# A Mamba-2 scan feeding a maxout FFN: decay rows laid out anew through DRAM, and the y matmuls of the seam in three portions

## The chip, the core and the metric

The kernel runs on one core of a Trainium2 chip. The core has TensorE (PE, matmuls), VectorE (DVE), ScalarE (ACT), GpSimd (POOL) and SyncE (SP), which here only issues DMAs; ScalarE issues a few as well. The engines run side by side and meet at semaphores. The metric is the device time of one execution in microseconds (us), lower is better: the median of the runs timed without the profiler. The profile is one further execution, with its own span.

## The reference

Two stages. The first is a scan over the sequence in chunks, with decays `a`; the second is a feed-forward layer with the maximum of three products.

```python
log_a = log(clip(a, 1e-6, 1))                        # a: (4 batches, 8 heads, 768)
for each chunk of the sequence:
    cum = cumsum(log_a in the chunk)
    L = exp(cum_i - cum_j) for i >= j, else 0
    y = ((C B^T) * L) x  +  (C state) * exp(cum)      # x: (4, 8, 768, 32); B, C: (4, 8, 768, 16)
    state = exp(sum of log_a) * state + sum_j B_j x_j exp(cum_last - cum_j)
t = y as (3072 tokens, 256)
h = max(t @ w1, t @ w2, t @ w3)                       # w: (256, 768)
out = h @ w_out                                       # (768, 256)
```

The kernel works in blocks of 128 tokens of all four batches and all eight heads: six blocks, c = 0 to 5. The blocks from c = 1 on are scanned in two halves (u) of 64 tokens. The index i is that of the token that receives, j that of the token that sends.

## The kernel before

At the start come small loads: block 0's decays (a0, four copies), B, C and x of block 0 and three pieces of the weights. The decays of all blocks (a_sb) are six loads on ScalarE's queue. They stand in the program after the logarithm of a0 and before fj0.

```python
a0 = const.tile([P, P], FP32, name="a0")
for k in range(REP):
    eng = nc.sync if k % 2 == 0 else nc.scalar
    eng.dma_start(out=a0[k * BH:(k + 1) * BH], in_=a_rows[:, 0:P])
a_sb = const.tile([R, 2, P], FP32, name="a_sb")          # R = 96 rows, twice
# ... activation table, loads, constants
spread_mask(b)                                            # b = 0, 1: first TensorE work
clip(cum0)                                                # cum0 is a0
lg0 = logs(cum0, "lg0")                                   # ScalarE: L264
for c in range(NC):
    w, k = divmod(c * BH, R)
    nc.scalar.dma_start(                                  # L378
        out=a_sb[k:k + BH, w], in_=a[:, :, c * P:(c + 1) * P].rearrange("b h i -> h b i"))
running(P, lg0, cum0, keep)                               # DVE scan: L269
# ...
fj0 = from_last(BH, cum0, "fj0")                          # ScalarE: L278
spread_i((0, 1), False)                                   # TensorE: L333
from_j[0] = by_token(BH, fj0, "from_j0", 1.0, ffn_bank)   # TensorE transpose: L287
spread_j((0, 1))                                          # TensorE: L345
```

The logarithms and running sums of a_sb go to DRAM (cums), and from there, copied to many partitions, to the decay matrices L (one for each block from c = 1) and to E (the decays that scale C and the states).

```python
scan_c(0)
lg = logs(a_sb, "lg")
running(R, lg, a_sb, keep2)
for w in range(2):
    nc.sync.dma_start(                                    # L960
        out=cums.rearrange("u c h b i -> u (c h b) i")[:, w * R:(w + 1) * R].rearrange(
            "u r i -> r u i"),
        in_=a_sb[:, w].rearrange("r (u i) -> r u i", u=2))
fetch()                                                   # a weight piece, 512 KB
decay_load(1, (0,))
fetch()
decay_load(1, (1,))
for _ in range(3):
    fetch()
load(1, "B")
load(1, "C")
fetch()
last_load(1)                                              # E
```

The masks (decay_masks, GpSimd, L406), exponentials (decay_part, ScalarE, L416) and products with the scores (scan_weight, DVE, L564) work on L with heads outside, batches inside. Then y of a block is made in two steps on TensorE, both of very short matmuls:

```python
def scan_old(c):                                          # L576: 32 matmuls
    # from the states (state of the block, and the middle state) and the scaled C
def scan_own(c):                                          # L592: 64 matmuls
    for b in range(NB):
        for h in range(NH):
            t, q = divmod(h, QH)
            for u in range(2):
                rows = slice(u * HP, (u + 1) * HP)
                nc.tensor.matmul(
                    out=st["y"][t][u][q * D:(q + 1) * D, b],
                    lhsT=st["x"][rows, b * NH + h], rhs=M[rows, h, b], ...)
```

The seam is the place between block 0 and the rest. The feed-forward of block 0 runs as 18 groups (n = 0 to 17), beside which the weights are decoded and block 1 is prepared. Then follow:

```python
for n in range(NF * 3):
    # ... one group of 2 matmuls 128x512 (L652), maximum on DVE (L1064), decode() and sign() of weights
    if n == 14:
        later.extend(scan_state(1, att_bank))             # the states, finished on GpSimd (L522)
    # ...
    if n == 17:
        decode()
        weight_sums(1)
shared["ffn"] = False
scan_old(1)
scan_own(1)
scan_y(1)                                                 # ScalarE copies y: L619
scan_sums(1)                                              # DVE sums of it: L627
pop(9)
transposed(2, False)                                      # trB: L435
scan_bd(2)
add_downs(0)
down_next()                                               # one output piece of block 0: L888
```

From there the feed-forward of a block c runs in nine steps, each of seven products 128x256 (L702; a Strassen form with sums on DVE), with the scan of block c + 1 in between.

Of the kernel before, what the change touches and what calls it, by code (L numbers as in the profile page):

```python
# [19 lines left out]
def kernel(  # L20
# [23 lines left out]
    nc = tc.nc  # L44
# [61 lines left out]
        eng.dma_start(out=a0[k * BH:(k + 1) * BH], in_=a_rows[:, 0:P])  # L106

    a_sb = const.tile([R, 2, P], FP32, name="a_sb")

    tabs = list(get_activation_tables(nc.m.arch).keys())  # L110
    nc.scalar.add_instruction(
# [187 lines left out]
        return scaled(turned(rows, src, name, bank), name, scale)  # L299

    L0 = att.tile([P, NB, NH, P], FP32, tag="L0", bufs=1, name="L0")
    Ls = {}

    def decays(c):
        Ls[c] = att.tile([P, NH, NB, HP], FP32, tag="L", name="L")
        return Ls[c]


# [62 lines left out]
    cum0 = a0.unsqueeze(1)  # L373
    clip(cum0)
    lg0 = logs(cum0, "lg0")
    for c in range(NC):
        w, k = divmod(c * BH, R)
        nc.scalar.dma_start(  # L378
            out=a_sb[k:k + BH, w], in_=a[:, :, c * P:(c + 1) * P].rearrange("b h i -> h b i"))
    running(P, lg0, cum0, keep)  # L380
    ncum[0] = by_token(BH, cum0, "ncum0", -1.0, ffn_bank)


    cums = dram.tile([2, NC, NH, NB, HP], FP32, name="cums")

    def decay_load(c, gs=(0, 1)):
        L = decays(c) if 0 in gs else Ls[c]
        for g in gs:
            h = slice(g * HALF, (g + 1) * HALF)
            for u in range(2):  # L390
                nc.sync.dma_start(
                    out=L[u * HP:(u + 1) * HP, h].rearrange("j h b i -> j (h b i)"),
                    in_=cums[u, c, h].rearrange("h b i -> (h b i)").partition_broadcast(HP))

    def last_load(c):
        E = blocks[c]["E"] = raw.tile([HN, 2, NB, HP], FP32, tag="E", name="E")
        for h in range(NH):
            nc.sync.dma_start(
                out=E[h * N:(h + 1) * N].rearrange("n u b i -> n u (b i)"),
                in_=cums[:, c, h].rearrange("u b i -> u (b i)").partition_broadcast(N))  # L400

    def decay_masks(c, g):

        h = slice(g * HALF, (g + 1) * HALF)
        for rows, base in ((P, HP), (HP, 0)):
            nc.gpsimd.affine_select(  # L406
                out=Ls[c][0:rows, h], in_=Ls[c][0:rows, h],
                pattern=[[0, HALF], [0, NB], [1, HP]], compare_op=ALU.is_ge, fill=MASKED,
                base=base, channel_multiplier=-1)

    def decay_part(c, r, b0):

        L = Ls[c]
        for b in (b0, b0 + 1):
            for h in (2 * r, 2 * r + 1):
                nc.scalar.activation(  # L416
                    L[:, h, b], L[:, h, b], AF.Exp,
                    bias=ncum[c][:, h * NB + b:h * NB + b + 1], scale=1.0)


    states = {}
# [43 lines left out]
    def scan_bd(c):  # L465
        st = blocks[c]
        st["Bd"] = Bd = att.tile([P, BH, N], FP32, tag="Bd", bufs=1, name="Bd")
        f = from_j[c].rearrange("p (b h) -> p b h", h=NH) if c == 0 else \
            from_j[c].rearrange("p (h b) -> p b h", b=NB)
        nc.gpsimd.tensor_tensor(  # L470
            out=Bd.rearrange("p (b h) n -> p b h n", h=NH),
            in0=st["B"].rearrange("p (b h) n -> p b h n", h=NH),
            in1=f.unsqueeze(3).to_broadcast([P, NB, NH, N]), op=ALU.mult)

    def first_state(kind):
        st = blocks[0]
# [83 lines left out]
        return banks  # L560

    def scan_weight(c, r, s):
        M = Ls[c][:, 2 * r:2 * r + 2].rearrange("p h b i -> p b h i")
        nc.vector.tensor_tensor(out=M, in0=s, in1=M, op=ALU.mult)  # L564

    def scan_old(c):
# [13 lines left out]
                        start=(b == 0), stop=False, tile_position=(r * PN, q),  # L580
                        skip_group_check=True)

    def scan_own(c):

        st = blocks[c]
        M = Ls[c]
        for b in range(NB):
            for h in range(NH):
                t, q = divmod(h, QH)
                for u in range(2):  # L590
                    rows = slice(u * HP, (u + 1) * HP)
                    nc.tensor.matmul(  # L592
                        out=st["y"][t][u][q * D:(q + 1) * D, b],
                        lhsT=st["x"][rows, b * NH + h], rhs=M[rows, h, b],
                        start=False, stop=True, tile_position=(u * HP, q * D),
                        skip_group_check=True)

# [83 lines left out]
    def weight_sums(k):  # L681
        q, i = divmod(k, 3)
        a11, a12, a21, a22 = (
            w_sb[i][:, kk, (2 * q + g) * P:(2 * q + g + 1) * P]
            for g in range(2) for kk in range(2))
        s1, s2, s3, s4 = (wsum[k][:, j] for j in range(4))
        nc.gpsimd.tensor_tensor(out=s1, in0=a21, in1=a22, op=ALU.add)
        nc.gpsimd.tensor_tensor(out=s3, in0=a11, in1=a21, op=ALU.subtract)
        nc.gpsimd.tensor_tensor(out=s2, in0=s1, in1=a11, op=ALU.subtract)
        nc.gpsimd.tensor_tensor(out=s4, in0=a12, in1=s2, op=ALU.subtract)  # L690
# [265 lines left out]
    scan_c(0)  # L956
    lg = logs(a_sb, "lg")
    running(R, lg, a_sb, keep2)
    for w in range(2):
        nc.sync.dma_start(  # L960
            out=cums.rearrange("u c h b i -> u (c h b) i")[:, w * R:(w + 1) * R].rearrange(
                "u r i -> r u i"),
            in_=a_sb[:, w].rearrange("r (u i) -> r u i", u=2))
    fetch()
    decay_load(1, (0,))
    fetch()
    decay_load(1, (1,))
    for _ in range(3):
        fetch()
    load(1, "B")  # L970
    load(1, "C")
# [29 lines left out]


    def decay_list(c):
        return [(c, r, b0) for r in range(NP) for b0 in (0, 2)]

    parts = {c: decay_list(c) for c in range(1, NC)}

# [5 lines left out]
    def first_tokens():  # L1013
        from_js = by_token(R, fj, "from_js", 1.0, att_bank)
        for c in range(1, NC):
            ncum[c], from_j[c] = (t[:, c * BH:(c + 1) * BH] for t in (ncums, from_js))

    def loads(c):
        if c < NC:
            if c == 3:  # L1020

                load(c, "x")
                decay_load(2, (1,))
                load(2, "x")
            decay_load(c)
            last_load(c)
            load(c, "B")
            load(c, "C")
            if c > 3:
                load(c, "x")  # L1030
# [10 lines left out]
    for n in range(NF * 3):  # L1041
        j, g = divmod(n, 2)
        q, i = divmod(j, 3)
        f = 2 * q + g
        if n == 0:
            pair = [ffn_bank([P, BLK], "up") for _ in range(2)]
            group(pair[0], 0, 0, (0,))
            first_own((2, 3))
            group(pair[1], 0, 1, (0,))
            for p, ff in zip(pair, range(2)):  # L1050
                group(p, 0, ff, (1,))
        if j > 0:
            p = ffn_bank([P, BLK], "up")
            whole_group(p, i, f)
        else:
            p = pair[g]
        if i == 0 and g == 0:
            m = ffn.tile([P, 4, HB], FP32, tag="m", name="m")
        pop({13: 2, 14: 1, 15: 2, 16: 1}.get(n, 0))
        mg = m[:, 2 * g:2 * g + 2].rearrange("p r t -> p (r t)")  # L1060
        if i == 0:
            nc.scalar.copy(out=mg, in_=p)
        else:
            nc.vector.tensor_tensor(  # L1064
                out=mg if i == 1 else h_of(0)[:, f], in0=mg, in1=p, op=ALU.max)
        if g == 0 and n <= 16:
            sign()
            if n <= 14:
                decode()
        if n == 1:  # L1070
            fj = from_last(R, a_sb, "fj", HP)
        if n == 3:
            first_tokens()
            load(2, "B")
            fetch()
            load(2, "C")
            fetch()
            decay_load(2, (0,))
            last_load(2)
            home(2, "x")  # L1080
            decay_masks(1, 0)
        if n == 5:
            decay_masks(1, 1)
        if n in (5, 7, 9, 10, 11, 12, 13, 14):
            part(1)
        if n == 11:
            transposed(1)
            scan_bd(1)
            scan_c(1)
        if n == 12:  # L1090
            scan_e(1)
            scan_cd(1)
            scores(1)
        if n == 14:
            later.extend(scan_state(1, att_bank))
        if n == 15:
            shared["att"] = False
            places()
            weight_sums(0)
        if n == 17:  # L1100
            decode()
            weight_sums(1)
    shared["ffn"] = False
    scan_old(1)
    scan_own(1)
    scan_y(1)
    scan_sums(1)
    pop(9)
    transposed(2, False)
    scan_bd(2)  # L1110
    add_downs(0)
    down_next()


# [4 lines left out]
    P1 = [(1, 0, 0), (1, 0, 0), (1, 0, 1), (1, 1, 1), (0, 0, 1), (1, 1, 2), (1, 0, 0), (1, 0, 2),  # L1119
          (1, 0, 2)]  # L1120
    D1 = [(0, 0), (0, 0), (2, 0), (2, 0), (2, 0), (2, 0), (0, 2), (0, 1), (0, 2)]
    K1 = {0: (0, 0), 1: (0, 1), 3: (1, 0), 5: (1, 1)}
    X2 = ["t", "s", "AD", "D", "D", "y", "D", "D", "D"]
    Y2 = ["", "", "", "D", "", "", "", "", ""]
    P2 = [(1, 0, 1), (1, 1, 2), (0, 0, 2), (1, 0, 1), (1, 0, 0), (1, 0, 0), (9, 0, 0), (1, 0, 0),
          (1, 0, 0)]
    D2 = [(0, 0), (2, 0), (1, 0), (0, 0)] + 5 * [(0, 1)]
    K2 = {2: (1, 0), 3: (1, 1)}
    X3, Y3, P3 = 9 * [""], 9 * [""], 9 * [(1, 0, 0)]

    for c in range(1, NC):
# [97 lines left out]
```

## Time and profile before

| | before |
|---|---|
| time, median of 3 | 311.21 us (311.11 to 311.37) |
| span of the profile | 311.2 us |
| TensorE busy | 287.4 us (92%), 3004 passes |
| VectorE busy | 208.3 us (67%) |
| ScalarE busy | 112.2 us (36%) |
| GpSimd busy | 121.9 us (39%) |
| moved by DMA | 23.02 MB, mean 74 GB/s |
| a_sb loads, ScalarE's queue | 6, of 16 KB |
| cums stores | 2, of 48 KB, 1.5 us to landing |
| decay loads (L from cums) | 20, of 256 KB, 5.2 us to landing |
| E loads (from cums) | 40, of 32 KB, 3.2 us to landing |

An engine's busy share is a mean over the span. The page also cuts the span into 40 slices of 7.8 us and gives the busy tenths of each; an empty slice of TensorE is worth more attention than the mean. The timeline gives for every instruction its start, its duration, and in brackets how long its engine had been idle and what released it. The chain of work that ended last goes back from the last instruction, at each step to what released it.

### The profile page before, as it was taken

The numbers are of one execution on the slowest core, as the hardware profiler recorded it, in microseconds if no ns is written. First come the engines' busy times: TensorE is split into PE (matmuls) and PEld (weight loads), VectorE is DVE, ScalarE is ACT, GpSimd is POOL, SyncE is SP. The second block draws the span as 40 slices with busy tenths as digits, with TensorE's granted clock in tenths as the row PEclk, the third lists the DMA queues.
The fourth block names the chain that finished last, engine by engine and source line by source line (L and its number), as shares of the span: only waits on it lengthen the run. The fifth ranks groups of instructions, "written<-read, shape, count | busy, mean of one in ns | idle before, by whom it ended". The sixth has DMA issues, their size and how long they took to land.

```text
span 311.2 us, 7425 instructions
## 1 busy us (share of the span) xinstructions
PE 287.4 (92%) x3004; PEld 230.5 (74%) x3004; DVE 208.3 (67%) x414; ACT 112.2 (36%) x335; POOL 121.9 (39%) x143
## 2 busy tenths in 40 slices
PE   5098998999699999999999999999999999999995
PEld 3075563445588888778898788898789878988885
DVE  2036448768376886987677678576886687586682
ACT  2037275692254553470333533342621211110111
POOL 4013328347549959193600293300625042130300
PEclk9999999999699999999999999999999999999999
DMA  8914997999577000279000478100100100000102
GB/s 84 231 44 118 214 211 161 176 206 147 71 171 74 29 3 2 87 149 106 19 19 2 134 113 95 38 2 0 36 2 0 38 0 34 3 0 0 36 1 101
DMA packets 84962, 23.02 MB, mean 74 GB/s; under 512 B 75904, under 2 KB 80576, under 8 KB 84928
## 3 DMA queue, kind: packets, MB, share of 16 engines
q1 hardware_dynamic: 84448, 22.29, 39.1%
q8 instruction: 23, 0.38, 0.5%
q10 hardware_dynamic: 480, 0.26, 0.3%
q14 instruction: 11, 0.09, 0.1%
HBM read 19.30 MB, written 3.24 MB: 72 GB/s over the span
## 4 chain that ended last, share of the span: by engine, by line
PE 79%; DVE 11%; DMA 2%; issue 2%; SPq 2%; ACT 1%; POOL 1%; ACTq 0%; DVEq 0%; POOLq 0%
PE sumB L702 24%; PE sumA L702 17%; PE o L812 13%; PE up L652 6%; PE o L888 3%; DMA raw_x<-in_x_dram 2%; PE y L592 2%; PE s L556 2%; PE s L537 2%; PE y L576 2%; DVE rb L627 2%; PE up L644 2%; DVE rb L744 1%; PE y L604 1%; PE spread L333 1%
## 5 line engine op out<-in xcount | busy, mean ns | idle before, releaser
L702 PE MATMUL sumA<-yT,w 128*128 128x256 f32 x180 | 55.5, 389 | 0.2
L787 POOL TENSOR_TENSOR hs<-h 128x256 f32<-128x256 f32 (+1 forms) x8 | 9.2, 1149 | 101.5 <-DVE h L747 101.5
L702 PE MATMUL sumB<-rb 128*128 128x256 f32 x180 | 46.7, 382 | 0.0
L727 ACT COPY eu<-sumA 128x256 f32<-128x256 f32 x45 | 16.8, 373 | 72.7 <-PE sumA L702 56.6
L416 ACT ACTIVATE L<-L,ncums 128x64 f32<-128x64 f32 x160 | 41.4, 340 | 4.0 <-POOL L L406 4.0
L702 PEld LDWEIGHTS sumB<-rb 128*128 128x128 f32 x180 | 34.7, 193 | 4.9
L702 PEld LDWEIGHTS sumA<-yT,w 128*128 128x128 f32 x180 | 31.0, 192 | 5.2 <-issue 1.0
L191 POOL TENSOR_TENSOR w_u<-w_u,w_r 128x512 uint32<-128x512 uint32 x12 | 15.2, 1270 | 39.6 <-DVE w_u L185 30.0
L652 PE MATMUL up<-yT,w 128*128 128x512 f32 x64 | 29.3, 601 | 1.5 <-DVE w L194 1.4
L744 DVE TENSOR_TENSOR rb<-sumB,eu 128x512 f32<-128x512 f32 x30 | 20.7, 692 | 12.6 <-PE sumB L702 12.4
L702 PE MATMUL sumB<-yT,rb 128*128 128x256 f32 x90 | 28.1, 393 | 1.2 <-DVE m L730 0.6
L728 DVE TENSOR_TENSOR eu<-sumA,eu 128x256 f32<-128x256 f32 x45 | 18.9, 421 | 15.1 <-ACT eu L727 14.8
L702 PE MATMUL sumA<-rb 128*128 128x256 f32 x90 | 27.2, 385 | 0.0
L702 PE MATMUL sumB<-rb,w 128*128 128x256 f32 x90 | 26.8, 379 | 0.0
L406 POOL TENSOR_SCALAR_AFFINE_SELECT L<-L 128x1024 f32<-128x1024 f32 (+1 forms) x20 | 24.7, 1233 | 0.7
L652 PEld LDWEIGHTS up<-yT,w 128*128 128x128 f32 x64 | 11.6, 190 | 15.9 <-issue 10.9
L729 DVE TENSOR_TENSOR v<-sumB,eu 128x256 f32<-128x256 f32 x45 | 19.1, 425 | 5.4 <-PE sumB L702 0.5
L702 PEld LDWEIGHTS sumB<-yT,rb 128*128 128x128 f32 x90 | 15.8, 189 | 7.6 <-DVE m L730 3.3
L702 PEld LDWEIGHTS sumA<-rb 128*128 128x128 f32 x90 | 17.4, 193 | 2.4
L702 PEld LDWEIGHTS sumB<-rb,w 128*128 128x128 f32 x90 | 17.1, 190 | 2.3
L812 PE MATMUL o<-wo,h 128*128 128x128 f32 x120 | 17.6, 280 | 0.6 <-DVE ob L821 0.6
L812 PEld LDWEIGHTS o<-wo,h 128*128 128x128 f32 x120 | 15.9, 191 | 2.8 <-ACT eu L727 1.1
(141 smaller groups left out, 507.8 us busy)
## 6 DMA issues: line engine op xcount, KB each, us to landing
L<-cums SPq DMA_DIRECT2D x20, 256.0 KB, 5.2
rb<-in_moe_w_dram SPq DMA_DIRECT2D x9, 512.0 KB, 8.4
raw_x<-in_x_dram SPq DMA_DIRECT2D x6, 512.0 KB, 6.6
out_dram<-ob SPq DMA_DIRECT2D x11, 256.0 KB, 2.2
raw_B<-in_B_dram SPq DMA_DIRECT2D x6, 256.0 KB
raw_C<-in_C_dram SPq DMA_DIRECT2D x6, 256.0 KB, 6.2
rb<-in_moe_w_out_dram SPq DMA_DIRECT2D x3, 512.0 KB, 6.0
E<-cums SPq DMA_DIRECT2D x40, 32.0 KB, 3.2
```

The source lines that it names most:

```text
L191: nc.gpsimd.tensor_tensor(out=u, in0=u, in1=r, op=ALU.add)
L406: nc.gpsimd.affine_select(out=Ls[c][0:rows, h], in_=Ls[c][0:rows, h], pattern=[[0, HALF], [0, NB], [1, HP]], compare_op=ALU.is_ge, fill=MA ...
L416: nc.scalar.activation(L[:, h, b], L[:, h, b], AF.Exp, bias=ncum[c][:, h * NB + b:h * NB + b + 1], scale=1.0)
L652: nc.tensor.matmul(out=bank, lhsT=w_sb[i][:, k, f * P:(f + 1) * P], rhs=yT[0][:, k], start=(k == 0), stop=(k == KD - 1))
L702: nc.tensor.matmul(out=bank[:, half], lhsT=left(p, k), rhs=sides[c][p], start=(first and half == 0), stop=True, skip_group_check=True)
L727: nc.scalar.copy(out=eu[:, 0], in_=A[:, 0])
L728: nc.vector.tensor_tensor(out=eu[:, 1], in0=A[:, 1], in1=eu[:, 0], op=ALU.add)
L729: nc.vector.tensor_tensor(out=v, in0=B[:, 1], in1=eu[:, 1], op=ALU.add)
L744: nc.vector.tensor_tensor(out=t[:, 0:2], in0=B, in1=eu[:, 1:2].to_broadcast([P, 2, HB]), op=ALU.add)
L787: eng.tensor_tensor(out=s1, in0=a21, in1=a22, op=ALU.add)
L812: nc.tensor.matmul(out=o[:, PLACES[p]], lhsT=token_sums[c][p][:, f, u], rhs=wo_of(p)[:, f], start=(p == first and f == 0), stop=True, skip ...
L888: nc.tensor.matmul(out=o[:, i], lhsT=hT[0][:, f, b * P:(b + 1) * P], rhs=wo_sb[:, f], start=(f == 0 and i == 0), stop=True, skip_group_che ...
```

## The change

Two things are changed.

The decay rows. a_sb is loaded in one transfer, ahead of the activation table, with batch and head outside and the block inside (row = (batch, head), block). For the layout that the decay loads need, the sums go to DRAM as they are (rows_dram) and two transfers from DRAM to DRAM, one for each half of a block, write cums anew. L now has batches outside and heads inside, so the decay loads, masks and exponentials go by pairs of batches instead of halves of the heads. The E loads take runs of 64 numbers instead of 256. The purpose is to free ScalarE's queue of the six loads, and to let scan_own begin with the first two batches.

The seam. scan_old(1) goes after group n = 16, scan_own(1) of batches 0 and 1 after n = 17, then one output piece of block 0, then scan_own(1) of batches 2 and 3. The short matmuls so stand in three portions with long ones in between. The number of matmuls stays; one output piece moves here from a later step.

```diff
     a_sb = const.tile([R, 2, P], FP32, name="a_sb")
+    nc.scalar.dma_start(
+        out=a_sb,
+        in_=a_rows.rearrange("r (c i) -> (r c) i", i=P).rearrange("(w r) i -> r w i", w=2))
...
-        Ls[c] = att.tile([P, NH, NB, HP], FP32, tag="L", name="L")
+        Ls[c] = att.tile([P, NB, NH, HP], FP32, tag="L", name="L")
...
-    for c in range(NC):
-        w, k = divmod(c * BH, R)
-        nc.scalar.dma_start(
-            out=a_sb[k:k + BH, w], in_=a[:, :, c * P:(c + 1) * P].rearrange("b h i -> h b i"))
     running(P, lg0, cum0, keep)
...
-    cums = dram.tile([2, NC, NH, NB, HP], FP32, name="cums")
+    rows_dram = dram.tile([BH, NC, P], FP32, name="rows_dram")
+    cums = dram.tile([NC, 2, NB, NH, HP], FP32, name="cums")
...
     def last_load(c):
...
-                out=E[h * N:(h + 1) * N].rearrange("n u b i -> n u (b i)"),
-                in_=cums[:, c, h].rearrange("u b i -> u (b i)").partition_broadcast(N))
+                out=E[h * N:(h + 1) * N].rearrange("n u b i -> n (u b) i"),
+                in_=cums[c, :, :, h].rearrange("u b i -> (u b) i").partition_broadcast(N))
...
-    def scan_own(c):
+    def scan_own(c, bs=range(NB)):
...
-    for w in range(2):
+    nc.sync.dma_start(
+        out=rows_dram.rearrange("k c s -> (k c) s").rearrange("(w r) s -> r w s", w=2), in_=a_sb)
+    fetch()
+    for u in range(2):
         nc.sync.dma_start(
-            out=cums.rearrange("u c h b i -> u (c h b) i")[:, w * R:(w + 1) * R].rearrange(
-                "u r i -> r u i"),
-            in_=a_sb[:, w].rearrange("r (u i) -> r u i", u=2))
+            out=cums[:, u].rearrange("c b h i -> c (b h) i"),
+            in_=rows_dram[:, :, u * HP:(u + 1) * HP].rearrange("k c i -> c k i"))
     fetch()
     decay_load(1, (0,))
     fetch()
-    decay_load(1, (1,))
-    for _ in range(3):
+    decay_load(1, (2,))
+    for _ in range(2):
         fetch()
...
+        if n == 16:
+            scan_old(1)
         if n == 17:
             decode()
             weight_sums(1)
+            scan_own(1, (0, 1))
     shared["ffn"] = False
-    scan_old(1)
-    scan_own(1)
+    add_downs(0)
+    down_next()
+    scan_own(1, (2, 3))
     scan_y(1)
     scan_sums(1)
     pop(9)
     transposed(2, False)
     scan_bd(2)
-    add_downs(0)
     down_next()
```

Left out of this cut: the same change of layout in the decay loads, masks, exponentials and the scaling of B; the order in which the parts of the exponentials are taken; and the tables of which mask runs in which step.

More of the change, by code (lines that the diff above doesn't have):

```diff
@@ L375, with decay_load @@
     lg0 = logs(cum0, "lg0")
-    for c in range(NC):
-        w, k = divmod(c * BH, R)
-        nc.scalar.dma_start(
-            out=a_sb[k:k + BH, w], in_=a[:, :, c * P:(c + 1) * P].rearrange("b h i -> h b i"))
     running(P, lg0, cum0, keep)
     ncum[0] = by_token(BH, cum0, "ncum0", -1.0, ffn_bank)
-    cums = dram.tile([2, NC, NH, NB, HP], FP32, name="cums")
[L386 to L389, printed above, removed]
+    rows_dram = dram.tile([BH, NC, P], FP32, name="rows_dram")
+    cums = dram.tile([NC, 2, NB, NH, HP], FP32, name="cums")
+    def decay_load(c, pairs=(0, 2)):
+        L = decays(c) if 0 in pairs else Ls[c]
+        for b in pairs:
             for u in range(2):
                 nc.sync.dma_start(
-                    out=L[u * HP:(u + 1) * HP, h].rearrange("j h b i -> j (h b i)"),
-                    in_=cums[u, c, h].rearrange("h b i -> (h b i)").partition_broadcast(HP))
+                    out=L[u * HP:(u + 1) * HP, b:b + 2].rearrange("j b h i -> j (b h i)"),
+                    in_=cums[c, u, b:b + 2].rearrange("b h i -> (b h i)").partition_broadcast(HP))
     def last_load(c):
@@ L398, in last_load, with decay_masks @@
             nc.sync.dma_start(
-                out=E[h * N:(h + 1) * N].rearrange("n u b i -> n u (b i)"),
-                in_=cums[:, c, h].rearrange("u b i -> u (b i)").partition_broadcast(N))
-    def decay_masks(c, g):
-        h = slice(g * HALF, (g + 1) * HALF)
+                out=E[h * N:(h + 1) * N].rearrange("n u b i -> n (u b) i"),
+                in_=cums[c, :, :, h].rearrange("u b i -> (u b) i").partition_broadcast(N))
+    def decay_masks(c, b0):
+        b = slice(b0, b0 + 2)
         for rows, base in ((P, HP), (HP, 0)):
             nc.gpsimd.affine_select(
-                out=Ls[c][0:rows, h], in_=Ls[c][0:rows, h],
-                pattern=[[0, HALF], [0, NB], [1, HP]], compare_op=ALU.is_ge, fill=MASKED,
+                out=Ls[c][0:rows, b], in_=Ls[c][0:rows, b],
+                pattern=[[0, 2], [0, NH], [1, HP]], compare_op=ALU.is_ge, fill=MASKED,
                 base=base, channel_multiplier=-1)
@@ L416, in decay_part @@
                 nc.scalar.activation(
-                    L[:, h, b], L[:, h, b], AF.Exp,
-                    bias=ncum[c][:, h * NB + b:h * NB + b + 1], scale=1.0)
+                    L[:, b, h], L[:, b, h], AF.Exp,
+                    bias=ncum[c][:, b * NH + h:b * NH + h + 1], scale=1.0)
     states = {}
@@ L467, in scan_bd @@
         st["Bd"] = Bd = att.tile([P, BH, N], FP32, tag="Bd", bufs=1, name="Bd")
-        f = from_j[c].rearrange("p (b h) -> p b h", h=NH) if c == 0 else \
-            from_j[c].rearrange("p (h b) -> p b h", b=NB)
         nc.gpsimd.tensor_tensor(
-            out=Bd.rearrange("p (b h) n -> p b h n", h=NH),
-            in0=st["B"].rearrange("p (b h) n -> p b h n", h=NH),
-            in1=f.unsqueeze(3).to_broadcast([P, NB, NH, N]), op=ALU.mult)
+            out=Bd, in0=st["B"], in1=from_j[c].unsqueeze(2).to_broadcast([P, BH, N]),
+            op=ALU.mult)
     def first_state(kind):
@@ L562, in scan_weight @@
     def scan_weight(c, r, s):
-        M = Ls[c][:, 2 * r:2 * r + 2].rearrange("p h b i -> p b h i")
+        M = Ls[c][:, :, 2 * r:2 * r + 2]
         nc.vector.tensor_tensor(out=M, in0=s, in1=M, op=ALU.mult)
@@ L581, in scan_old @@
                         skip_group_check=True)
-    def scan_own(c):
+    def scan_own(c, bs=range(NB)):
         st = blocks[c]
         M = Ls[c]
-        for b in range(NB):
+        for b in bs:
             for h in range(NH):
@@ L593, in scan_own @@
                         out=st["y"][t][u][q * D:(q + 1) * D, b],
-                        lhsT=st["x"][rows, b * NH + h], rhs=M[rows, h, b],
+                        lhsT=st["x"][rows, b * NH + h], rhs=M[rows, b, h],
                         start=False, stop=True, tile_position=(u * HP, q * D),
@@ L1003, in decay_list @@
     def decay_list(c):
-        return [(c, r, b0) for r in range(NP) for b0 in (0, 2)]
+        return [(c, r, b0) for r, b0 in (
+            (0, 0), (1, 0), (0, 2), (1, 2), (2, 0), (2, 2), (3, 0), (3, 2))]
     parts = {c: decay_list(c) for c in range(1, NC)}
@@ L1015, in first_tokens @@
         for c in range(1, NC):
-            ncum[c], from_j[c] = (t[:, c * BH:(c + 1) * BH] for t in (ncums, from_js))
+            ncum[c], from_j[c] = (
+                t.rearrange("p (k c) -> p c k", c=NC)[:, c] for t in (ncums, from_js))
     def loads(c):
@@ L1022, in loads @@
                 load(c, "x")
-                decay_load(2, (1,))
+                decay_load(2, (2,))
                 load(2, "x")
@@ L1082 @@
         if n == 5:
-            decay_masks(1, 1)
+            decay_masks(1, 2)
         if n in (5, 7, 9, 10, 11, 12, 13, 14):
@@ L1121 @@
     D1 = [(0, 0), (0, 0), (2, 0), (2, 0), (2, 0), (2, 0), (0, 2), (0, 1), (0, 2)]
-    K1 = {0: (0, 0), 1: (0, 1), 3: (1, 0), 5: (1, 1)}
+    K1 = {0: (0, 0), 1: (0, 2), 3: (1, 0), 5: (1, 2)}
     X2 = ["t", "s", "AD", "D", "D", "y", "D", "D", "D"]
@@ L1127 @@
     D2 = [(0, 0), (2, 0), (1, 0), (0, 0)] + 5 * [(0, 1)]
-    K2 = {2: (1, 0), 3: (1, 1)}
+    K2 = {2: (1, 0), 3: (1, 2)}
     X3, Y3, P3 = 9 * [""], 9 * [""], 9 * [(1, 0, 0)]
```

## The prediction

> **What bounds the kernel now.** I read the page's row of engines and its forty slices first, then TensorE's waits, then the timeline around the two largest of them, then a table by stage. TensorE is busy 287.4 of 311.2 us; only its 24 us of idleness, and the time in which it runs slowly, can be won.
>
> The slices and the instruction queues of the page, and TensorE's waits, longest first in total:
>
> ```profile
> PE   5098998999699999999999999999999999999995
> PEclk9999999999699999999999999999999999999999
> DMA  8914997999577000279000478100100100000102
> q8 instruction: 23, 0.38, 0.5%
> q14 instruction: 11, 0.09, 0.1%
> ```
>
> ```profile
> PE from_j_tp L287 <- ACT fj L278: 8.9, 1, 8.9
> PE y L592 <- issue: 3.2, 1, 3.2
> PE spread L317 <- DVE keep L254: 2.5, 1, 2.5
> PE up L652 <- DVE w L194: 1.4, 2, 1.1
> ```
>
> Slice 1 (7.8 to 15.6 us) is empty on TensorE, and slice 10 (78 to 86 us) is the only later one below 8; its clock digit is also the only low one. The waits name both: 8.9 us for an exponential on ScalarE, and 3.2 us at the y matmuls, put down to nothing ("issue"). From slice 11 on TensorE is full, so what is won before about 87 us should move the end by as much.
>
> Why ScalarE is late shows in its timeline (start, duration, then the instruction; ACTq is its DMA issuing; from several windows, so the x3 and x2 rows share one issue):
>
> ```profile
> 3.74 0.31 ACT L264 ACTIVATE lg<-a 128x128 f32<-128x128 f32 x1 [0.71 <-DVE a L259]
> 3.75 2.69 ACTq L378 DMA_DIRECT2D a_sb<-in_a_dram  x3
> 5.76 1.39 ACTq L378 DMA_DIRECT2D a_sb<-in_a_dram  x2
> 10.87 0.67 ACTq L378 DMA_DIRECT2D a_sb<-in_a_dram  x1
> 14.47 0.67 ACTq L378 DMA_DIRECT2D a_sb<-in_a_dram  x1
> 15.19 0.40 ACT L278 ACTIVATE fj<-a 32x128 f32<-32x128 f32 x1 [11.14 <-DMA a_sb<-in_a_dram]
> ```
>
> ScalarE computes nothing from 4.05 to 15.19 us, although its input, the scan of a0, is ready at 4.50 (L269: 4.08 + 0.42). Six small loads of a_sb stand before fj in its program, and the fifth and sixth are held back. The chain of work that ended last says by what: it has the landing of raw_x (7.01 + 7.44 = 14.45), then this issue at 14.47, fj, and the transpose at 15.64. The program's order with its waits agrees: DMAs of both queues take eight completion semaphores in turn, and the sixth a_sb load waits for that of raw_x, the fifth for that of the first weight piece. No bandwidth of its own is missing.
>
> The stages (us; busy time and count of PE, PEld, DVE, ACT, POOL; granted clock; DMA share; GB/s):
>
> ```profile
> 6.74:15.64 8.90, 0.00 (x1) 0.00 (x0) 0.00 (x0) 0.40 (x1) 0.57 (x1) 1.00 1.22 224
> 38.00:75.00 37.00, 35.48 (x238) 17.13 (x234) 27.16 (x44) 25.11 (x65) 18.07 (x16) 1.00 1.01 178
> 77.20:80.40 3.20, 0.04 (x6) 0.04 (x8) 0.00 (x0) 0.00 (x0) 3.12 (x5) 0.90 0.24 55
> 80.40:87.00 6.60, 6.33 (x43) 5.11 (x44) 2.77 (x5) 2.93 (x8) 2.04 (x4) 0.53 0.82 124
> ```
>
> In the second hole DVE and ScalarE are idle too and DMA is almost so. Then TensorE runs 6.6 us at about half clock.
>
> [...] 0.38 MB in 23 packets is 16.5 KB each. An fp32 matmul here is four instructions (two weight loads, two passes), a transpose two. Counting TensorE's program up to the hole, I get 869 before the y stage, 128 for scan_old, and 102 passes with their 102 loads of scan_own: 1201. [...] the hole lies amid scan_own, at no wait of the program, with every other engine's input ready. [...] For the SP-issued cums store of before the trace shows 1.5 us to landing. [...] no run shows the new transfers yet.
>
> **Part 1, decay rows.** Six a_sb loads (11.40 us of ScalarE's queue) become one of 96x2x128, issued after the two a0 loads at about 1.7 us. Those took 0.91 together, so I allow 0.5. The table load (1.28) then ends about 3.5, and the log waits for DVE's clip (3.71) anyway: 0 to 0.6 lost, say 0.2. fj runs at about 4.7 instead of 15.19. TensorE finishes its 32 spread passes at 6.74 and takes from_j_tp at once: 8.9 - 0.2 = 8.7 us earlier. Are the next inputs there 8.7 us earlier? From the bytes by microsecond, raw_B and raw_C are in by about 8.0 us, the first weight piece by 10.3, raw_x by 14.45, two more weight pieces by 16.4. The first needs, moved forward: trB 10.8, trC 13.8, first weight decode 16.4, state product 20.0. All hold, the decode by 6 us.
>
> The layout costs DMA work. Before: two cums stores at 25.71, landing in 1.5, then decay loads at 27.27. After: a rows_dram store at about 17, a weight piece behind it, two DRAM-to-DRAM transfers after its landing (about 19), and the decay loads after theirs (about 22 behind the weight piece) instead of 18.6 in moved time: 3 to 4 us later. Their mask runs on GpSimd at 47.22, moved 38.5, so 12 us are left. Weight pieces 4 to 9 also shift 1 to 2 us, with the same sort of slack (piece 4 issued 26.61, decoded 43.86). The final scaling loads E change from 1 KB to 256-byte runs, 1024 instead of 256 per block. raw_x moved 4096 runs of 128 bytes in about 4 us, so by proportion about 1 us; E is issued at 46.98 and used at 66.66. Hidden. ScalarE's exponentials (160 at 340 ns), masks and scan weights keep number and size. Net: -8.7, less 0.2 for small slips.
>
> **Part 2, y at the seam.** TensorE's order becomes: groups up to n=16, scan_old, group 17, half of scan_own, one output piece, the other half. Nothing is added; one output piece is taken from a later slot. In before's clock: groups 15 and 16 end at 73.1. scan_old then waits for the middle state, which GpSimd finishes at 74.62: about 1.5 us of new wait. Then 1.1 (scan_old), 1.8 (group, four passes), 0.7 (half of scan_own, half of the 1.41 a later block took), 0.9 (piece), 0.7: the end of y at 79.8 [...] Left over: 0.6, y ends at 80.4, against 81.0 before with one piece fewer done (0.86: four passes at 0.216, as eight took 1.73 at 95.57). The hole being short, the clock stays up. Then four ScalarE copies and DVE's four sums (80.86 to 84.0, 3.1 us) still stand before the products; they end at about 83.8 instead of 87.0. Seam: 3.2 + 0.86 = 4.1 us if all works. I count 2.7, since [...] DVE (5.0 of 5 us busy from 70 to 75) may take over.
>
> **Sum.** 311.2 - 8.5 - 2.7 = 300.0 us.
>
> **Rivals.** (a) The early hole is only partly filled: a_sb's issue is slowed beside raw_B's 4096 runs, or the weight stream takes over between 38 and 75 us. For: DMA ran at 178 GB/s there, and before it rested from 16.5 to 25.7, a rest that vanishes. Against: only 1.4 us of waits for decoded weights, and 6 us or more of slack. Gain 4 to 6 instead of 8.7: 303 to 305. (b) The seam stays: [...] the wait for GpSimd grows. Gain 0 there, perhaps -1: 302.7 to 304. For: GpSimd is busy 3.12 of 3.20 us in the hole and sets the middle state. (c) All works and TensorE also warms sooner, since it starts continuous work at 2.5 instead of 15.6: 296 to 298. Against: from 15.64 to about 37 it was almost always busy and its 128x128 transposes still took 0.28 us each (1.11 for four at 19.46), against 0.15 when warm (0.60 for four at 86.97), so the small row tiles seem not to warm it. (d) The extra DRAM hop starves the decay path and costs more than all this: over 311; nothing in the slack speaks for it.
>
> **Range and chances.** (a) or (b) alone stay under 305, the 2% line; both together come to about 307. Range 296.5 to 304.0; faster by over 2% 0.92, within 0.07, slower 0.01.
>
> **What would show it.** Right: slice 1 of TensorE full, fj at about 4.7 us and from_j_tp near 6.9; rows_dram at about 17; decay masks near 38.5 with no DMA wait; TensorE waiting about 1.5 us at scan_old for GpSimd; no slow-clock slice near 70 us. Wrong: fj early but a wait for weights or raw_x taking its place; the "issue" wait of 3 us again among the y matmuls with the clock falling after it; or later slices no longer full.

## The result and the profile after

| | before | changed |
|---|---|---|
| time, median of 4 (us) | 311.16 | 293.42 (292.81 to 294.15) |
| ratio, 95% interval | | 0.943 (0.9406 to 0.9455) |
| span of the profile (us) | 311.2 | 292.4 |
| TensorE busy (us) | 287.4 | 277.6 |
| from_j_tp starts (us) | 15.64 | 6.37 |
| first 128x512 group starts | 41.47 | 23.82 |
| scores of block 2 start (chain) | 101.18 | 82.30 |
| from there to the end of the span | 210.0 | 210.1 |

The change is 17.7 us faster, not 11.2. 300.0 was predicted, with 296.5 as the lower end. The last row says that nothing came from later than 101 us. The third row from below says that 17.65 of the 18.8 us of span were won before 41.47 us, where 8.5 were expected.

The slices of the page after (tenths busy, granted clock, DMA share):

```profile
PE   6899899888999989999999999999999999999995
PEclk9999999999999999999999999999999999999999
DMA  7969989979980007871005971001001001000103
```

No slice of TensorE is empty and the slow slice at the seam is gone. TensorE's waits after, longest first in total:

```profile
PE spread L319 <- DVE keep L257: 2.5, 1, 2.5
PE up L648 <- DVE w L197: 1.4, 2, 1.1
...
PE y L572 <- POOL S L518: 1.2, 1, 1.2
PE o L884 <- DVE wo L197: 1.1, 1, 1.1
...
PE y L588 <- issue: 0.4, 1, 0.4
```

The waits of 8.9 and 3.2 us are gone. Two new ones stand at the seam: scan_old for GpSimd's state (1.2, foreseen as 1.5), and an output piece for its decoded weight (1.1, not foreseen).

That waits alone do not explain it shows when the same work is put side by side. TensorE's timeline of the changed kernel (start, duration):

```profile
4.40 2.17 PE L335 MATMUL spread<-a,pick 32*128 32x128 f32 x32
8.03 1.52 PE L335 MATMUL spread<-a,pick 32*128 32x128 f32 x16
9.48 0.66 PE L434 MATMUL trB<-ident,raw_B 128*128 128x128 f32 x4
19.06 1.13 PE L640 MATMUL up<-yT,w 128*128 128x256 f32 x4 [0.70 <-ACT yT L607]
```

and of the kernel before:

```profile
4.57 2.17 PE L333 MATMUL spread<-a,pick 32*128 32x128 f32 x32
17.52 2.01 PE L333 MATMUL spread<-a,pick 32*128 32x128 f32 x16
19.46 1.11 PE L435 MATMUL trB<-ident,raw_B 128*128 128x128 f32 x4
34.88 2.08 PE L644 MATMUL up<-yT,w 128*128 128x256 f32 x4 [0.70 <-ACT yT L611]
```

trB is 9.98 us earlier, the first up matmul 15.82: many of the matmuls between them run almost twice as fast. In what follows, warm is TensorE at full granted clock, cold at half. At 4.4 us it is cold in both kernels: the same 32 passes take 2.17 us in both. In the changed kernel single passes of `spread` shrink from 416 ns to 270 between 8.3 and 8.9 us, so it is warm from about 8.7 us on instead of about 38.8. The page's clock digits do not show it: both read 9 from the start. The clock record of the changed kernel's trace begins only at 8.71 us and that of before at 38.82; what lies ahead of the record is printed as full.

In some executions of experiments 4 to 6 the mean granted clock was lower (0.971 to 0.988) and the time 3 to 7 us longer; where single times are named these are left out or named apart.

### The profile page after: what moved, and what is told of

The parts are those of the page before. It is cut to its first block, busy times and chain, and to the rows that moved or that the text cites. A ratio compares the mean times of both kernels' runs of the same rounds, so it can differ in the third digit from the quotient of the medians.

```text
span 292.4 us, 7409 instructions
## 1 busy us (share of the span) xinstructions
PE 277.6 (95%) x3004; PEld 223.2 (76%) x3004; DVE 207.8 (71%) x414; ACT 112.1 (38%) x335; POOL 121.8 (42%) x143
## 4 chain that ended last, share of the span: by engine, by line
PE 71%; DVE 12%; DMA 8%; SPq 3%; ACT 2%; issue 2%; POOL 1%; DVEq 0%; ACTq 0%; POOLq 0%
PE sumB L698 25%; PE sumA L698 17%; PE o L808 14%; PE o L884 3%; SPq L134 3%; PE y L588 3%; DMA L<-cums 2%; DMA rb<-in_moe_w_dram 2%; PE y L572 2%; PE s L552 2%; DVE rb L623 2%; DMA rows_dram<-a_sb 1%; DVE L L560 1%; DVE rb L740 1%; PE spread L335 1%
## 5 line engine op out<-in xcount | busy, mean ns | idle before, releaser
L698 PE MATMUL sumA<-yT,w 128*128 128x256 f32 x180 | 54.9, 386 | 0.3 <-DVE eu L724 0.2
L698 PEld LDWEIGHTS sumB<-rb 128*128 128x128 f32 x180 | 34.1, 190 | 5.0 <-DVE rb L623 0.4
L405 POOL TENSOR_SCALAR_AFFINE_SELECT L<-L 128x1024 f32<-128x1024 f32 (+1 forms) x20 | 26.0, 1299 | 0.7
```

The lines of the kernel that those rows point to most:

```text
L405: nc.gpsimd.affine_select(out=Ls[c][0:rows, b], in_=Ls[c][0:rows, b], pattern=[[0, 2], [0, NH], [1, HP]], compare_op=ALU.is_ge, fill=MASKE ...
L698: nc.tensor.matmul(out=bank[:, half], lhsT=left(p, k), rhs=sides[c][p], start=(first and half == 0), stop=True, skip_group_check=True)
```

## The experiments

**1. Is it the clock? The hole filled, in the kernel before.**

```diff
     fj0 = from_last(BH, cum0, "fj0")
     spread_i((0, 1), False)
+    filler = bank("sumB", 2, [P, HALF, P], "filler")
+    for _ in range(34):      # never read
+        nc.tensor.matmul(out=filler.rearrange("p k i -> p (k i)"), lhsT=ident16,
+            rhs=mask.unsqueeze(1).to_broadcast([P, HALF, P]), start=True, stop=True, ...)
     from_j[0] = by_token(BH, fj0, "from_j0", 1.0, ffn_bank)
```

> The kernel before, with 34 filler matmuls 128x512 bf16 on TensorE in the hole ahead of from_j_tp; nothing else moves, ScalarE still reaches fj at about 15.2 us. Clock theory: TensorE is warm when the hole ends, the stretch from from_j_tp to the first up matmul shrinks from 19.2 us to about 12.5, and the time falls by about 7 us, to 304. Rival (the extra gain comes from transfers or other engines that now start earlier): no change, 311. Block theory of the seam: the 68 added instructions move the hole among the y matmuls of scan_own from after 102 passes to after 68; if it is a wait for data it stays after 102.

No interval could be had: the four times are 303.53, 309.6, 310.8 and 314.78 us, beside 308.01 to 313.38 for before. Their mean granted clocks, in the same order, are 0.999, 0.978, 0.971 and 0.956. The profiled execution, the longest of them, tells why. Its stages, TensorE alone (us; busy and count; granted clock; DMA share; GB/s):

```profile
6.40:13.60 7.20, 7.18 (x34) 1.00 1.27 181
13.60:15.75 2.15, 0.00 (x0) 1.00 1.04 332
15.75:16.00 0.25, 0.25 (x5) 0.68 1.08 401
17.00:36.00 19.00, 16.94 (x146) 0.50 0.45 113
39.00:40.00 1.00, 1.00 (x3) 0.63 1.05 385
```

The fill ended 2.15 us too soon, for it ran warm (0.21 us each; the four 128x512 bf16 passes at 2.54 us of the kernel before take 1.86 together). The clock had fallen within 0.25 us of from_j_tp's start (0.68 in that row) and stayed at half until about 39.7 us, although TensorE was busy for 16.94 of the 19 us from 17 to 36. So the cold stretch is real, and this trace, unlike the two before, dates it (that of the seam-only kernel in experiment 5 has it on record too, with no fill). The fastest execution (303.53, mean clock 0.999) is where the clock theory put it, but one execution shows little.

The block theory, which has the place of the hole go with the number of instructions ahead of it on TensorE, had no trace behind it. Its forecast failed as put: the hole in scan_own did not move to 68 passes. It vanished (128 passes in 1.49 us at 76.44), and three later y stages, untouched by the edit, got one each:

```profile
118.08 0.45 PE L592 MATMUL y<-L,raw_x 64*32 64x64 f32 x28 [1.45 <-issue]
198.68 0.42 PE L592 MATMUL y<-L,raw_x 64*32 64x64 f32 x23 [1.73 <-issue]
245.43 0.41 PE L592 MATMUL y<-L,raw_x 64*32 64x64 f32 x19 [1.55 <-issue]
```

They come after 100, 105 and 109 of the 128 passes; before's came after 102. From 112 to 120 us DMA's share was 0.01, so busy DMA is not needed for such a hole.

**2. The hole put back into the changed kernel.** ScalarE copies a small tile onto itself 34 times ahead of fj.

```diff
+    slow = const.tile([P, 64], FP32, name="slow")
+    nc.gpsimd.memset(slow, 0.0)
+    for _ in range(34):
+        nc.scalar.activation(slow, slow, AF.Copy)
     fj0 = from_last(BH, cum0, "fj0")
```

> The changed kernel, with 34 small ScalarE operations ahead of fj that hold it back by about 9 us, so the early hole is back while every transfer stays as changed. Clock theory: TensorE stays cold to the first up matmuls, cost 9 + 7 = 16 us, time about 309. Rival: cost only the 9 us, about 302.

314.4 us (313.7 to 314.85), 21 us over the changed kernel; from_j_tp at 17.31, 10.9 us later. TensorE's timeline shows the slow durations of before again:

```profile
21.13 1.11 PE L434 MATMUL trB<-ident,raw_B 128*128 128x128 f32 x4
36.55 2.08 PE L640 MATMUL up<-yT,w 128*128 128x256 f32 x4 [0.70 <-ACT yT L607]
```

The first 128x512 group starts 19.7 us later than in the changed kernel: 10.9 for the hole and 8.8 beyond. All of the transfers' new order was kept, so the new order of the transfers does not bring those 8.8 us.

**3. Held back and filled.** The same with 50 fill matmuls as in experiment 1.

> The changed kernel with fj held back as in the run before (a hole of about 10.8 us) and the hole filled by 50 matmuls 128x512 bf16 on TensorE. Clock theory: TensorE stays warm, only the 10.8 us are lost, 304 us, ten less than without the fill (314.4). Rival (the rest of the cost of holding fj back is in transfers or other engines): about 314 again.

313.31 us, the median of 20 executions from 308.97 to 318.56: near the rival's 314, but not for the rival's reason. Up to the scores of block 2 it was what the clock theory says: they start at 91.94, against 101.76 held without fill. Afterwards it lost the same again. TensorE's waits of this kernel begin:

```profile
PE y L588 <- issue: 6.0, 4, 2.0
```

Three holes of 1.8 to 2.0 us and one of 0.3, in y stages that had none when fj was held without fill, and the mean clock fell to 0.988. The fill adds 100 instructions and nothing else to TensorE's program.

**4. Filled with 256 instructions.** The fills of 68 and 100 instructions came with new holes in y stages. Here the fill is 128 short matmuls, 256 instructions with a load and a pass each; why this number should do better is not shown. For the held kernel (104 columns twice) and for the kernel before (90 columns twice):

```diff
+    for _ in range(128):
+        nc.tensor.matmul(out=filler[:, 0:2, 0:104], lhsT=ident16,
+            rhs=mask[:, 0:104].unsqueeze(1).to_broadcast([P, 2, 104]), start=True, stop=True, ...)
```

> As the held and filled kernel before, but with 128 short fill matmuls, 256 instructions[...]. Clock and block theory together: the hole of about 11 us costs only itself, 304 to 305 us, and no y stage gets a new hole over 0.6 us. Rival to the block theory (the four late holes of the 50-matmul fill came from something else): holes of 1.5 to 2 us again and about 313.

304.25 and 304.38 us: ten less than held without fill, by useless work on TensorE alone (the other two executions took 310.29 and 310.24, at mean clocks of 0.978 and 0.977). Its timeline:

```profile
20.04 0.66 PE L434 MATMUL trB<-ident,raw_B 128*128 128x128 f32 x4
29.61 1.13 PE L640 MATMUL up<-yT,w 128*128 128x256 f32 x4 [0.70 <-ACT yT L607]
```

No y stage waits for "issue" now; one such wait of 0.9 stands at a sumB product.

> The kernel before with the early hole filled by 128 short matmuls, 256 instructions, up to the moment at which ScalarE delivers fj (from_j_tp still at about 15.7 us). Clock theory: the stretch from from_j_tp to the first 128x512 group shrinks from 25.8 to about 17.5 us and the time falls by 7 to 8.4 us against before. Block theory: the hole of the seam stays where it was, after about 102 passes, and no other y stage gets one. Rival: no change.

302.23 to 302.78 us (a fourth execution took 309.16, at a mean clock of 0.971); ratio to before 0.9713 (0.9679 to 0.9748), with from_j_tp no earlier than before (17.05, the fill overran by a little). The hole at the seam is back in its place, after 101 passes, as the only one of the y stages:

```profile
67.90 1.20 PE L592 MATMUL y<-L,raw_x 64*32 64x64 f32 x101
70.64 0.44 PE L592 MATMUL y<-L,raw_x 64*32 64x64 f32 x27 [1.54 <-issue]
```

The clock runs in one table (us):

| kernel | from_j_tp | from there to the first 128x512 group | time |
|---|---|---|---|
| before | 15.64 | 25.83 | 311.2 |
| before, filled (256) | 17.05 | 16.35 | 302.5 |
| changed | 6.37 | 17.45 | 293.4 |
| changed, held | 17.31 | 26.20 | 314.4 |
| changed, held and filled (256) | 18.03 | 16.35 | 304.3 |

The middle column has two levels, about 26 and about 17, and what chooses between them is whether TensorE was at work just before. At the lower level the changed kernel needs 1.1 us more than the filled ones, which are warm when from_j_tp starts; it is not yet.

**5. The two parts one by one.** The changed rows with the seam of before, and the kernel before with the changed seam (moving the four calls as the diff of the change does, and nothing else).

> The changed decay rows with the seam of before (scan_old, scan_own whole after group 17, output pieces after trB). Theory that most of the seam's gain is given back (the pulled-forward pieces meet a weight that is not decoded): 1 to 1.5 us slower than the changed kernel, about 294.6, with a hole of about 3 us after 102 passes of scan_own and a slow clock after it. Rival (the seam is worth what was predicted): 296 to 297.5.

293.1, 294.46 and 294.97 us (a fourth execution took 298.97); ratio 0.9453 (0.9406 to 0.9499). The hole comes after 103 passes, but is 1.9 us instead of 3.2:

```profile
58.19 1.23 PE L588 MATMUL y<-L,raw_x 64*32 64x64 f32 x103
61.33 0.43 PE L588 MATMUL y<-L,raw_x 64*32 64x64 f32 x25 [1.91 <-issue]
```

The clock then is 0.50 from about 63.1 to 66.5.

> The kernel before with only the seam changed. Given-back theory: 1 to 1.5 us faster than before, about 310. Rival: 307 to 308.5. In both the early hole of 8.9 us and the cold stretch after it stay.

311.74 us; ratio to before 1.0024 (0.9994 to 1.0053): nothing, less than either theory. Its trace shows the cold stretch of the kernel before without any fill (TensorE alone; the columns are those of experiment 1):

```profile
6.25:8.00 1.75, 0.00 (x0) 1.00 1.25 133
9.00:9.50 0.50, 0.00 (x0) 0.73 0.55 164
9.50:10.00 0.50, 0.00 (x0) 0.50 1.05 410
15.78:38.00 22.22, 20.16 (x171) 0.50 0.53 120
40.00:41.00 1.00, 1.00 (x6) 1.00 1.05 387
```

Half clock is on record from 9.2 us, inside the early hole, until about 40, busy or not. What it was ahead of 9.2 is not shown: there the view prints full. Once more side by side, on one chip:

> The changed kernel itself, beside the rows-only kernel on the same chip: 293 to 294 us under every theory.

> Changed decay rows, seam of before, again beside the changed kernel. Theory that the seam's gain is given back in full (as the seam alone, which was worth nothing): within 0.5 us of the changed kernel. Rival (seam worth 1 us or more): 294.5 or more while the changed kernel stays at 293.5.

Changed 292.38, 293.07, 293.49, 294.0; rows only 293.24, 293.71, 293.87, 295.0 (two more of each, left out, took 296.79 to 300.43). Half a microsecond between the medians (293.28 and 293.79), with ranges that overlap. The seam is worth 0.5 us here, if anything; in the kernel before it was worth nothing.

**6. Where the seam's gain went.** TensorE's timeline of the changed kernel at the seam: two portions of y, and the third output piece.

```profile
56.99 1.04 PE L572 MATMUL y<-Cd,S 32*64 32x64 f32 x56 [1.17 <-POOL S L518]
61.73 0.57 PE L588 MATMUL y<-L,raw_x 64*32 64x64 f32 x35
62.67 0.45 PE L588 MATMUL y<-L,raw_x 64*32 64x64 f32 x29 [0.37 <-issue]
68.56 1.13 PE L884 MATMUL o<-wo,h 128*128 128x256 f32 x4 [1.14 <-DVE wo L197]
```

The hole shrank to 0.37, after 35 passes of the half. But 1.17 are paid for the state. The third piece, pulled forward by one step, waits 1.14 for the second piece of w_out. To test this, the piece is left out of step 0 of block 1, so the queue of pieces runs one step later:

```diff
             elif x == "tc":
                 scan_tc(n, att_bank)
-                down_next()
```

> The changed kernel without the output piece in step 0 of block 1, so the third piece comes one step later, when its weight is decoded, and a later step does the twelfth. Theory (the pulled-forward third piece waits 1.1 us for the decoding and so gives back what the seam won): the wait is gone, about 292.3. Rival (the piece is work that must be done somewhere, and the wait only moves): 293.4, unchanged.

291.91, 292.16, 292.63 and 293.05 us (two more took 296.24 and 297.21), 0.9 below the changed kernel by median (292.4 and 293.28), with ranges that overlap. The wait is gone. TensorE's timeline from trB to the scores of block 2, of the changed kernel on that chip:

```profile
62.30 0.66 PE L434 MATMUL trB<-ident,raw_B 128*128 128x128 f32 x4 [0.38 <-ACT yT L615]
67.49 1.13 PE L884 MATMUL o<-wo,h 128*128 128x256 f32 x4 [1.50 <-DVE wo L197]
81.15 1.21 PE L552 MATMUL s<-CT,BT 32*64 32x128 f32 x64
```

and with the piece later:

```profile
63.24 0.66 PE L434 MATMUL trB<-ident,raw_B 128*128 128x128 f32 x4 [0.38 <-ACT yT L615]
80.16 1.21 PE L552 MATMUL s<-CT,BT 32*64 32x128 f32 x64
```

That is 18.85 and 16.92 us. The edit does two things in this stretch: the wait of 1.50 goes, and one piece (0.86) moves behind the scores, from where on both kernels take 210.1 us. So the gain at the seam is not the wait's alone, and of these 1.93 us the piece-later trace had lost 0.94 before trB. Again:

> The piece-later kernel again on the same chip: 292.4 to 292.8.

291.12, 291.87 and 292.09 (three more took 297.05 to 297.42); ratio to before 0.9366 (0.9332 to 0.9401). This is the fastest of the versions tried. It keeps both parts of the change.

A further try moved scan_old behind group 17, with one piece on either side of the first half of scan_own.

> The variant with the piece later, and scan_old moved behind group 17, with an output piece on either side of the first half of scan_own and none after trB. The wait of 1.2 us for GpSimd's middle state should vanish; [...] the hole in scan_own should grow from 0.4 to about 1. If both are right: 0.3 to 0.6 us below the piece-later kernel, about 292.2; if the filler missing after trB costs as much, the same.

The best two of six executions took 293.14 and 293.48, the other four 296.56 to 297.01: slower than piece-later on the same chip. The wait for the state vanished and the hole grew to 1.07, both as expected. But the missing filler let TensorE wait 0.8 for DVE's sums, and after these two waits the clock fell to half from about 65.2 to 68.6:

```profile
62.35 0.46 PE L588 MATMUL y<-L,raw_x 64*32 64x64 f32 x33 [1.07 <-issue]
...
65.11 1.14 PE L698 MATMUL sumA<-rb 128*128 128x256 f32 x2 [0.81 <-DVE rb L623]
```

## Why the prediction was wrong, step by step

- **What bounds it** held. Time won before 87 us moved the end one for one: from block 2's scores to the end it is 210.0 us before and 210.1 after.
- **Part 1, the hole**: right. Forecast 8.7, measured 9.27 (15.64 to 6.37). fj came at 4.37 instead of about 4.7: the one load took 0.45 of the queue, and a0 landed a little earlier.
- **Part 1, the term that was missing.** "The first needs, moved forward: trB 10.8, trC 13.8 ..." carried the whole stretch forward with the durations it had. They were cold durations. Up to the first 128x512 group the gain is 17.65: 9.27 for the hole and 8.4 for the clock, a term set at zero. This is the step that failed. Experiment 2 takes this gain away (8.8 us) and experiment 4 gives it back (9.85 us) without changing a transfer.
- **Rival (c)** named this and was put down because from 15.64 to 37 TensorE was almost always busy and yet cold. The observation was right and the inference was not. That the work after 15.64 us does not warm a cold TensorE (experiment 1: 16.94 of 19 us busy, clock 0.50) says neither that the work ahead of it does not, nor that a warm TensorE goes cold in it. In the changed kernel TensorE works from 2.54 us to 11.8 without a break, the clock rises at 8.71, and from there the same small tiles run at full clock (16 passes of `spread` at 10.07 take 1.16 us, against 2.08 at 20.50 before). The rival was also sized too small: 296 to 298 is a gain of 2 to 4 us over 300, where the clock brought 8.4.
- **The DMA work of the layout**: hidden, as said, though it takes longer than I put it. The rows_dram store went out at 14.21 and landed after 4.25 us, where about 2 were put down (17 to 19); cums took 2.56 more; the first decay loads left at 21.10. That is 6.9 us behind the store, against 1.6 before, so 5.3 later where 3 to 4 were forecast. The masks ran at 29.57 straight after other work, with no wait for DMA. The E loads landed in 3.8 us at the median instead of 3.2. The slack is smaller than it looks, though: the chain of work that ended last now runs through these transfers (the store at 14.21, cums at 18.48, L at 21.10, then the queue and two weight pieces to 46.90). It comes back to TensorE only at scan_old, in the wait of 1.17 us for the state.
- **Part 2**: the parts were nearly right and the sum was not. Wait for the state 1.2 (forecast 1.5), hole left over 0.4 (0.6, an estimate; what makes the hole is not shown), at 35 passes of the half. The clock stayed up, as forecast: 1.00 from 60 to 70 us, beside waits of 0.37 and 1.14. Forecast 2.7 in all; measured 0.5 with changed rows and none with the old ones. Two terms were missing. The moved piece was counted as 0.86 saved, but its old place cost nothing (210.0 and 210.1), so it was only work put into the seam. And pulling the queue forward met a weight not yet decoded, 1.1 to 1.5 us. Experiment 6 takes both away at once: 1.93 us less between trB and the scores, 0.9 in the time. In addition the hole that the portions remove is 1.9 us with the changed rows, not 3.2.
- **The "issue" wait at the seam**: no trace shows its cause. In these runs holes came and went with the number of instructions ahead. With 68 added to the kernel before, the one after 102 passes vanishes and three appear in later y stages (1.45 to 1.73 us). With 100 added to the held kernel, three of 1.8 to 2.0 us and one of 0.3 appear. With 256 added, the hole of the kernel before stands after 101 passes, and the held kernel has none in a y stage. The forecast for 68, a hole after 68 passes, failed, and the length of a hole (1.5 to 3.2 us) is not explained.

## What to carry to other kernels

A hole in TensorE's time can cost more than its length, as here (8.8 us beyond 10.9, experiment 2), where small-tile work follows it: look up the durations of the same matmuls warm and cold, and ask which of the two will hold once the hole is gone. Count instructions when very short matmuls stand in a dense run: adding 68 or 100 far ahead opened holes there, and adding 256 to the kernel before left its hole in place. When work is moved forward as a filler, check that what it reads is ready one step sooner, and that its old place cost anything.

## What was not expected of the hardware

- The work behind the hole, most of it small tiles, did not raise the clock: in experiment 1 it was 16.94 of 19 us, at 0.50. In the kernel before, the up matmuls (128x256, full array) begin at 34.88 and the clock is up from 38.82; in experiment 1 it is up near 39.7. It is not the small shape alone: in the changed kernel the clock rose at 8.71 us, 4.3 us after the last full-array matmul, with only row tiles (32 rows) in between. There 32 passes took 2.17 us, behind the hole 16 of the same form 2.01, both cold. Which work counts for the rise is open.
- The clock fell 2.6 us into the hole of 3.2 at the seam of the kernel before, at most 2.3 us after the fill of experiment 1 ended, and 1.7 us after the 1.9 us hole of rows-only was over, with work already running again. In the seam-only kernel half clock is on record from 3.0 us after the last work. The slow stretch that followed was 3.4 us long in rows-only (63.1 to 66.5) and in the further try (65.2 to 68.6), and twice that in the kernel before (79.8 to 86.6).
- Two useless fills that differ in length and number (50 matmuls, 128 short ones) differ by 9 us in the time of the kernel, 313.3 and 304.3, at the same stretch of 16.35 us in the place where they stand.
